# Half-row products of batches 2 to 7: stages A, D and C in one stretch each, with a value bank as the fourth place

## The chip, the cores and the metric

The program runs on one core of one Trainium2 chip. The metric is device time in microseconds, one execution at a time, as the median of the runs shown.

## The reference

```python
def _attn_ref(x):                       # x: 8 x 3072 x 256
    X = np.fft.fft(x, axis=1)
    X = np.fft.fft(X, axis=2)
    return X.real.astype(np.float32)

def _moe_ref(x, mu_k, mu_r, w_k, w_v, w_r):
    x_prev = np.concatenate([np.zeros((B, 1, D)), x[:, :-1, :]], axis=1)
    xk = mu_k * x + (1.0 - mu_k) * x_prev
    xr = mu_r * x + (1.0 - mu_r) * x_prev
    k = np.maximum(xk @ w_k, 0.0)
    v = k * k @ w_v
    return (1.0 / (1.0 + np.exp(-(xr @ w_r)))) * v
```

The output of the first function is the x of the second: a two-dimensional Fourier transform of each batch, of which the real part is kept, and then a channel mix with a squared ReLU (width 1024) and a sigmoid gate.

## The kernel before

**The main loop.** The channel mix of all eight batches is cut into 48 chunks of 512 positions, six to a batch, and each chunk into four steps, so that a batch has 24 steps. A step holds `k_piece` (four products of 512 columns with `wk`, line 825, then a ReLU by ACT, line 835), one `v_tile` (eight products of 256 columns with `wv`, line 866) and, every fourth step, `r_item` (eight products with `wr`, line 852, then a sigmoid by ACT). DVE squares the ReLU's result at every second step (line 845) and multiplies a finished value tile by the gate (`v_out`, line 888), which goes out by DMA.

**The transform of the next batch** is woven into these steps, in three stages. Stage A multiplies the folded input by a table `w_h` and makes `a`. Stage D multiplies `a` by `w_d` and makes `g_all`. Stage C multiplies `g_all` by `m_cs` and makes `pq`; DVE adds and subtracts its halves (`halves`). From batch 2 on (stage D: from batch 3 on) the products of these stages take only half of TensorE's rows: 48 or 64 of 128 rows, the lower half (`lo64`) or the upper one (`hi64`). They are issued alternately, lower and upper, and write different banks of one tile.

**PSUM.** Three tiles of two banks each (`psW0` to `psW2`, handed out in turn by `ps_w`) serve `k_piece`, `r_item` and all three stages; two tiles of one bank each (`psV0`, `psV1`, `ps_v`) serve the value tiles. A value bank takes two value tiles, `tb` 0 and 1 or `tb` 2 and 3, and is free when `v_out` has read it. A `psW` tile is free when ACT has copied it out (`evac`, line 574).

**The order** is written out by hand. `at(step, f, ...)` puts work at a step; `event(step, ...)` puts half-row products behind that step's `v_tile`; `v_behind(steps)` moves the `v_tile` of these steps up, ahead of their own `k_piece`. A step runs thus: `k_piece`, the small stage work, `v_tile`, the event, a `v_tile` that was moved up, DVE's `v_out` if the step stands in `OUT_FIRST`, the DVE work, `v_out` otherwise, the square. Every engine runs its instructions in exactly this order. For batch t of 3 to 7, with s = 24t - 48, the half-row products stand in four **stretches**, each between two stretches of ordinary 128-row products:

- s+29: the 2 leading products of stage A (line 603, all rows) and 46 half-row products (line 617), in three `psW` tiles
- s+33: 48 half-row products of stage D (line 679), three tiles
- s+37: the last 4 of stage D and 32 of stage C (line 746), three tiles
- s+41: 24 of stage C, and the first 16 of stage A of batch t+1, two tiles

Batch 2 has its own steps: 16 products of its stage A stand in a stretch at step 20 that stays for batch 1's stage C; then come stretches at 31 (A), 39 (C) and 41 (C, and batch 3's first 16 of A). Its stage D uses all rows.

Of the kernel before, what the change touches and what calls it, by code (L numbers as in the profile page):

```python
# [9 lines left out]
FP32 = mybir.dt.float32  # L10
FP16 = mybir.dt.float16
# [28 lines left out]
def kernel(  # L40
# [23 lines left out]
    y_pool = ctx.enter_context(tc.tile_pool(name="y_sb", bufs=1))  # L64
# [15 lines left out]

    def ps_v():
        return ps_slot("V", 2, 512)
# [22 lines left out]
    xp_t, xm_t, p_t, eo_t = {}, {}, {}, {}  # L105
    V = nc.vector
# [175 lines left out]
    lo64, hi64 = slice(0, 64), slice(64, 128)  # L282
# [15 lines left out]
    g_all = const.tile([P, NU // 2, 256], FP16)  # L298
# [4 lines left out]
    m_cs = const.tile([P, 3, NJ, 64], FP16)  # L303
# [81 lines left out]
    WA, WB = 4 * NU, 2 * NU  # L385
# [3 lines left out]
    w_h, w_h0 = w_hh[:, 0:WB], w_hh[:, WB:2 * WB]  # L389
# [150 lines left out]
    w_d = const.tile([P, 2, 64], FP16)  # L540
# [25 lines left out]
    a_t = {}  # L566
    y_t = {}
    x_t = {}

    def evac(out_ap, in_ap, eng):  # L570
        if eng == "V":
            V.tensor_copy(out=out_ap, in_=in_ap)
        else:
            nc.scalar.activation(out=out_ap, in_=in_ap, func=AF.Copy)  # L574

    def a_tile(b):
        a_t[b] = y_pool.tile([P, 2, NU, 64], FP16, name="a")
# [20 lines left out]

    def a_slot_0(b, e):
        a_ps[b, 1, e] = ps_w()
        nc.tensor.matmul(out=a_ps[b, 1, e][:, 2 * NU * 7:2 * NU * 8], lhsT=eo_t[b, 0][0:112, 0, e, :],
                         rhs=w_h0, start=True, stop=True)

    def a_slots_0(b):
        for e in range(2):
            a_slot_0(b, e)

    def a_half(b, h, e, eng="A"):  # L610
        if (h, e) == (0, 0):
            a_tile(b)
        ps = a_ps[b, h, e] if h else ps_w()
        for i in range(8):
            for g in range(h and i == 7, 2):
                rows = slice(64 * g, 64 * g + N1)
                nc.tensor.matmul(out=_v(ps, 512 * g + 2 * NU * i, [(1, 2 * NU)]),  # L617
                                 lhsT=eo_t[b, h][rows, i + 1 - h, e, :], rhs=w_h[rows],
                                 start=True, stop=True)
        evac(_v(a_t[b], 64 * NU * e + 8 * h, [(16, 2), (32, 2 * NU), (1, 8)]),  # L620
             _v(ps, 0, [(512, 2), (1, 2 * NU), (2 * NU, 8)]), eng)

    def a_sum(b, h, i0, eng="A", m=4):

# [19 lines left out]
    a_ps = {}  # L644
# [24 lines left out]
        d_units(b, ps, 4 * n, k, 512)  # L669
        d_evac(ps, 4 * n, k, 512, eng)  # L670

    def d_half(b, n, eng="A"):
        u0, k = 4 * n, min(4, NU // 2 - 4 * n)
        ps = ps_w()
        for i in range(k):
            for e in range(2):
                for g, rows in enumerate((lo64, hi64)):
                    o = 512 * g + 256 * e + 64 * i
                    nc.tensor.matmul(out=ps[:, o:o + 64],  # L679
                                     lhsT=a_t[b][rows, e, 2 * (u0 + i):2 * (u0 + i) + 2, :],  # L680
                                     rhs=w_d[rows, e], start=True, stop=True)
        evac(_v(g_all, 256 * u0, [(1, 2), (128, 2 * k), (2, 32)]),
             _v(ps, 0, [(512, 2), (32, 2 * k), (1, 32)]), eng)
        evac(_v(g_all, 256 * u0 + 64, [(128, 2), (256, k), (1, 64)]),
             _v(ps, 256, [(512, 2), (64, k), (1, 64)]), eng)

    def d_small(b, u, n, eng="A"):
        ps = ps_v()
# [34 lines left out]
    def c_tiles(b):  # L723
        y_t[b] = y_pool.tile([P, NSL + 1, 2, 64], FP16, name="y")
# [13 lines left out]
    def c_pairs(b, s0, n, eng="A"):  # L738
        if s0 == 0:
            c_tiles(b)  # L740
            y_t[b, "pq"] = y_pool.tile([P, 2 * NJ, 2, 64], FP16, name="pq")
        ps = ps_w()
        for f in range(2):
            for sl, i, rows, u in c_slots(s0, n):
                o = 512 * (sl % 2) + 128 * i + 64 * f
                nc.tensor.matmul(out=ps[:, o:o + 64], lhsT=g_all[rows, u, 128 * f:128 * f + 128],  # L746
                                 rhs=m_cs[rows, f, sl // 2], start=True, stop=True)
        evac(_v(y_t[b, "pq"], 128 * s0, [(256, n // 2), (128, 2), (1, 128)]),
             _v(ps, 0, [(128, n // 2), (512, 2), (1, 128)]), eng)

    def halves(b, lo, hi, hs=(0, 1)):
# [189 lines left out]
    w, first = ps_w(), ps_w()  # L941
# [15 lines left out]
    for a in range(2):  # L957
        t = x_t["t", a] = mix_pool.tile([P, 24, 64], FP16, name=f"t{a}")
# [8 lines left out]
    odd = ps_v()  # L967
# [14 lines left out]
    work = {}  # L982

    def at(step, f, *args):
        work.setdefault((step, "x" if f in (a_item, a_sum, d_item, d_small, c_item, c_tiles, turned, minus_0, r_item, quarter_tables) else "w"),
                        []).append((f, args))


# [76 lines left out]
    at(16, fold, 2, 0)  # L1065
    at(17, butterfly, 2, 0)
    event(18, (c_pairs, 1, 0, 8, "V"), (c_pairs, 1, 8, 8))
    event(20, (c_pairs, 1, 16, 8), (c_pairs, 1, 24, 4), (a_half, 2, 0, 0))
    v_behind(21)
    at(19, halves, 1, 0, 13)  # L1070
    at(20, diff, 1, 0, 12)
# [48 lines left out]
    for t in range(3, B):  # L1120
        s = 24 * t - 48

        def every(step, f, *args):
            at(s + step, f, t, *args)

        every(9, fold, 0)
        every(12, quarters_1, 0)
        every(13, quarters_2, 0)
        every(15, fold, 1)
        every(26, quarters_1, 1)  # L1130
        every(27, quarters_2, 1)
# [29 lines left out]
    for step in range(nk + LAG):  # L1161
# [3 lines left out]
        v = v_steps.get(step)  # L1165
# [52 lines left out]
```

## Time and profile before

| | |
|---|---|
| time, median of 3 runs | 427.71 us (427.27 to 428.07) |
| span of the profiled execution | 425.4 us |
| TensorE busy | 419.5 us (99%), granted clock 0.999 |
| DVE busy | 371.4 us (87%) |
| ACT busy | 327.2 us (77%) |

The profile is of one execution. Its span runs from the first to the last instruction; the measured time holds some 2.3 us more, which lie outside the span. In the views, a line such as L679 is a line of the kernel, `out<-in` names tiles, xN counts instructions, and "DVE" or "ACT" behind an arrow is the engine that ended a wait. A row of the chain of waits gives a start, a length and the instructions that held the end of the program during it.

### The profile page before, as it was taken

What the parts mean: (1) busy time and instruction counts of PE and PEld (TensorE: products, weight loads), DVE (VectorE), ACT (ScalarE), POOL (GpSimd) and SP (SyncE); (2) the same over time, 40 slices, a digit from 0 to 9 for tenths busy, and PEclk for the clock granted to TensorE, in tenths of its full rate; (3) what the DMA queues carried; (4) which work ended last, traced back from release to release, by engine and by line L of the source; (5) the groups of instructions that cost most, each with busy time, mean ns of one, the idle gap of its engine ahead of it and who ended that gap; (6) DMA issues with size and microseconds to landing.
All of it is one profiled execution on the core that took longest, in us unless ns stands there. A gap on an engine that the chain in (4) does not pass through costs nothing.

```text
span 425.4 us, 9649 instructions
## 1 busy us (share of the span) xinstructions
PE 419.5 (99%) x3991; PEld 294.6 (69%) x3991; DVE 371.4 (87%) x593; ACT 327.2 (77%) x407; POOL 64.3 (15%) x99
## 2 busy tenths in 40 slices
PE   8999999999999999999999999999999999999996
PEld 3767766776677767776767676777767776776765
DVE  8999999999998989989899898988899776977553
ACT  7889886797867986689767887678876798666661
POOL 7478500200060001400041000500000000000000
PEclk9999999999999999999999999999999999999999
DMA  8779972632385233932349232772223232332334
GB/s 173 109 118 185 228 158 57 117 87 55 73 161 137 52 76 57 217 97 51 75 79 216 55 73 55 140 169 57 68 59 74 54 74 52 74 70 55 76 74 101
DMA packets 35104, 42.08 MB, mean 99 GB/s; under 512 B 4114, under 2 KB 31092, under 8 KB 35060
## 3 DMA queue, kind: packets, MB, share of 16 engines
q1 hardware_dynamic: 27488, 25.41, 24.6%
q0 software_dynamic: 7264, 15.80, 21.5%
q8 instruction: 31, 0.51, 0.5%
q10 hardware_dynamic: 308, 0.26, 0.2%
q14 instruction: 13, 0.11, 0.1%
HBM read 32.08 MB, written 25.17 MB: 135 GB/s over the span
## 4 chain that ended last, share of the span: by engine, by line
PE 98%; DVE 1%; issue 0%; POOL 0%; ACT 0%; POOLq 0%
PE psW L825 39%; PE psV L866 37%; PE psW L852 10%; PE psV L878 3%; PE psW L746 2%; PE psW L617 1%; PE psW L679 1%; PE psW L235 1%; PE psW L635 1%; PE psW L657 1%; PE psV L378 1%; PE psW L714 0%; DVE rw L308 0%; PE psV L657 0%; PE psV L635 0%
## 5 line engine op out<-in xcount | busy, mean ns | idle before, releaser
L835 ACT ACTIVATE rl<-psW 128x1024 f16<-128x1024 f32 x192 | 193.7, 1032 | 82.3 <-PE psW L825 81.2
L825 PE MATMUL psW<-x,wk 128*128 128x512 f16 (+1 forms) x776 | 193.4, 377 | 0.3 <-DVE x L962 0.3
L866 PE MATMUL psV<-wv_sb,k 128*128 128x256 f16 x1424 | 184.3, 273 | 0.0
L866 PEld LDWEIGHTS <-k 128*128 128x128 f16 x1424 | 136.4, 98 | 38.3
L845 DVE TENSOR_TENSOR k<-rl 128x2048 f16<-128x2048 f16 (+1 forms) x100 | 115.6, 1157 | 26.3 <-ACT rl L835 26.0
L825 PEld LDWEIGHTS <-wk 128*128 128x128 f16 x776 | 75.6, 98 | 54.9 <-issue 0.4
L888 DVE SCALAR_TENSOR_TENSOR o<-psV,r 128x512 f32<-128x512 f32 (+1 forms) x97 | 65.7, 680 | 15.0 <-PE psV L866 14.1
L790 DVE TENSOR_TENSOR x<-y,t 128x1536 f16<-128x1536 f16 (+3 forms) x76 | 62.4, 827 | 2.2
L857 ACT ACTIVATE r<-psW 128x1024 f16<-128x1024 f32 x48 | 49.5, 1032 | 0.8 <-PE psW L852 0.8
L852 PE MATMUL psW<-wr,x 128*128 128x256 f16 x384 | 49.8, 273 | 0.0
L852 PEld LDWEIGHTS <-x 128*128 128x128 f16 x384 | 37.5, 98 | 14.2 <-issue 0.2
L574 ACT ACTIVATE g_all<-psW 128x512 f16<-128x512 f32 (+8 forms) x62 | 29.0, 542 | 1.3 <-PE psW L679 1.0
L574 ACT ACTIVATE a<-psW 128x832 f16<-128x832 f32 x31 | 25.4, 865 | 1.2 <-PE psW L617 1.2
L494 POOL IOTA gate<- 1x1 int32 x7 | 0.8, 121 | 163.8 <-DVE gate L493 163.8
L574 ACT ACTIVATE pq<-psW 128x1024 f16<-128x1024 f32 (+1 forms) x27 | 23.3, 917 | 1.5 <-PE psW L746 1.4
L141 POOL DMA_INDIRECT xm<-in_x_dram,idx_g x18 | 23.5, 1304 | 5.5 <-issue 5.5
L779 DVE TENSOR_SCALAR t<-d,muf_t 128x1536 f16<-128x1536 f16 (+3 forms) x44 | 21.8, 508 | 0.1
L172 DVE TENSOR_TENSOR p<-xp,xm 112x2304 f16<-112x2304 f16 (+6 forms) x19 | 21.7, 1141 | 0.1
L779 DVE TENSOR_SCALAR t<-d,mu_m 128x1536 f16<-128x1536 f16 x32 | 19.6, 612 | 0.0
L759 DVE TENSOR_TENSOR y<-pq 128x960 f16<-128x960 f16 (+3 forms) x28 | 15.8, 604 | 3.2 <-ACT pq L574 2.8
L767 DVE TENSOR_TENSOR d<-y 128x1664 f16<-128x1664 f16 (+5 forms) x19 | 16.7, 879 | 0.3 <-ACT y L574 0.2
L878 PE MATMUL psV<-wv_sb,k 128*128 128x256 f16 x112 | 14.7, 273 | 0.0
(148 smaller groups left out, 221.1 us busy)
## 6 DMA issues: line engine op xcount, KB each, us to landing
out_dram<-o SPq DMA_DIRECT2D x189, 128.0 KB, 2.4
xp<-in_x_dram POOLq DMA_DIRECT2D x12, 216.0 KB, 4.4
xp<-in_x_dram POOLq DMA_DIRECT2D x13, 192.0 KB, 6.9
xp<-in_x_dram POOLq DMA_DIRECT2D x2, 384.0 KB, 8.0
wv_sb<-in_moe_w_v_dram POOLq DMA_DIRECT2D x1, 512.0 KB, 8.3
xp<-in_x_dram SPq DMA_DIRECT2D x1, 480.0 KB, 4.2
xp<-in_x_dram POOLq DMA_DIRECT2D x1, 432.0 KB
xm<-in_x_dram,idx_g POOLq DMA_INDIRECT x18, 9.2
```

The lines of the kernel that those rows point to most:

```text
L141: nc.gpsimd.indirect_dma_start(dst, None, src, bass.IndirectOffsetOnAxis(ap=idx, axis=0))
L574: nc.scalar.activation(out=out_ap, in_=in_ap, func=AF.Copy)
L779: V.tensor_scalar(out=dst, in0=src, scalar1=mu, scalar2=None, op0=ALU.mult)
L790: V.tensor_tensor(out=_v(x_t[b, j, m], o, [(64 * step, hi - lo), (step, 64)]), in0=y_t[b][:, lo + 3 * m:hi + 3 * m, a], in1=x_t["t", a][:, ...
L825: nc.tensor.matmul(out=st["k", ds][:, 512 * hs + lo:512 * hs + hi], lhsT=wk_sb[m][a][:, 128 * fc:128 * fc + 128], rhs=xk[:, a, 512 * i + l ...
L835: nc.scalar.activation(out=st["rl"][:, 2 * ds:2 * ds + 2], in_=st["k", ds].rearrange("p (f t) -> p f t", f=2), func=AF.Relu, bias=0.0, sca ...
L845: V.tensor_tensor(out=k2_t[c][:, lo:hi], in0=r, in1=r, op=ALU.mult)
L852: nc.tensor.matmul(out=ps[:, 256 * tb:256 * tb + 256], lhsT=x_t[b, 1, m][:, a, 512 * i + 128 * tb: 512 * i + 128 * tb + 128], rhs=wr_sb[m] ...
L857: nc.scalar.activation(out=st["r", c], in_=ps, func=AF.Sigmoid)
L866: nc.tensor.matmul(out=st["v", tb - h][:, 256 * h:256 * h + 256], lhsT=k2_t[c][:, fc, 128 * tb:128 * tb + 128], rhs=wv_sb[:, fc], start=(f ...
L878: nc.tensor.matmul(out=st["v", tb - h][:, 256 * h:256 * h + 256], lhsT=k2_t[c][:, fc, 128 * tb:128 * tb + 128], rhs=wv_sb[:, fc], start=fc ...
L888: V.scalar_tensor_tensor(out=o.rearrange("p a b -> p (a b)")[:, 0:256 * n], in0=st["v", t0][:, 0:256 * n], scalar=16.0, in1=st["r", c][:, ...
```

## The change

Each of the stages A, D and C of a batch gets one stretch: A (62 products) at s+29, D (52) at s+33, C (54) at s+37; the stretch at s+41 goes, and so does batch 2's at 41. One stage needs more than three `psW` tiles hold, so the rest of its products goes to a fourth place, the value bank that is not being filled at that time (`v_bank`). That bank is taken without moving the count that hands out value banks, so the next pair of value tiles gets the same bank. The products that write its lower-half part stand first in the stretch, and are copied out during it; those of its upper-half part stand last, and are copied out third, ahead of the last `psW` tile. All these copies are ACT's. The two leading products of stage A (`a_slot_0`) move to an earlier step, in a tile of their own with an evacuation of their own. The two products for a slot of stage C that is not used are left out, and `turned` runs once a batch and not in two parts. `v_out` moves ahead of the other DVE work at the steps s+28, s+32, s+36 and at step 30.

```diff
+    def v_bank():
+        k = ps_n["V"] % 2
+        return psum.tile([P, 512], FP32, name=f"psV{k}", tag=f"psV{k}", bufs=1)
+
+    def side_by_side(lo, hi, n, f):
+        for k in range(max(len(lo), len(hi))):
+            if k == n:
+                f()
+            for items in (lo, hi):
+                for out, w, r in items[k:k + 1]:
+                    nc.tensor.matmul(out=out, lhsT=w, rhs=r, start=True, stop=True)
...
+        lo, hi = both(0), both(1)
+        side_by_side(run(v, 0, 0, 1, 12, 15) + lo,
+                     hi + run(v, 3 * WB, 1, 1, 12, 16) + run(v, 7 * WB, 1, 0, 15, 16),
+                     3, lambda: out(v, 0, 1, 12, 3, (0,)))
+        out(ws[0], 0, 0, 0, 9)
+        out(ws[1], 0, 1, 0, 9)
+        out(v, 3 * WB, 1, 12, 4, (1,))
+        out(v, 7 * WB, 0, 15, 1, (1,))
+        out(ws[2], 0, 0, 9, 6)
+        out(ws[2], 6 * WB, 1, 9, 3)
...
+    def d_all(b):
+        ws = [ps_w() for _ in range(3)]
+        v = v_bank()
...
+        def out(ps, n, k, gs=(0, 1), o=0, e=256):
+            g, m = gs[0], len(gs)
+            evac(_v(g_all, 1024 * n + g, [(1, m), (128, 2 * k), (2, 32)]),
+                 _v(ps, o, [(512, m), (32, 2 * k), (1, 32)]), "A")
+            evac(_v(g_all, 1024 * n + 64 + 128 * g, [(128, m), (256, k), (1, 64)]),
+                 _v(ps, o + e, [(512, m), (64, k), (1, 64)]), "A")
+
+        side_by_side(run(0, 3) + run(0, 0) + run(0, 1) + run(0, 2),
+                     run(1, 0) + run(1, 1) + run(1, 2) + run(1, 3),
+                     2, lambda: out(v, 3, 1, (0,), 0, 64))
+        out(ws[0], 0, 4)
+        out(ws[1], 1, 4)
+        out(v, 3, 1, (1,), 128, 64)
+        out(ws[2], 2, 4)
...
+        side_by_side(run(1, 3) + run(1, 0) + run(1, 1) + run(1, 2),
+                     run(0, 0) + run(0, 1) + run(0, 2) + run(0, 3), 2,
+                     lambda: evac(_v(pq, 128 * 25, [(1, 128)]), _v(v, 128, [(1, 128)]), "A"))
+        out(0)
+        out(1)
+        evac(_v(pq, 128 * 24, [(256, 2), (1, 128)]), _v(v, 0, [(256, 2), (1, 128)]), "A")
+        out(2)
...
-    OUT_FIRST = (12, 20, 28, 36, 38, 40)
+    OUT_FIRST = (12, 20, 28, 30, 36, 38, 40, *(24 * t - 48 + k for t in range(3, B) for k in (28, 32, 36)))
...
-    event(31, (a_slots_0, 2), (a_half, 2, 1, 0), (a_half, 2, 1, 1), (a_half, 2, 0, 1))
+    at(22, a_slot_0, 2)
+    event(31, (a_all, 2))
...
-    event(39, (c_pairs, 2, 0, 8), (c_pairs, 2, 8, 8))
-    event(41, (c_pairs, 2, 16, 8), (c_pairs, 2, 24, 4), (a_half, 3, 0, 0))
-    v_behind(42)
+    event(39, (c_all, 2))
+    v_behind(40)
...
-        event(s + 29, (a_slots_0, t), (a_half, t, 1, 0), (a_half, t, 1, 1), (a_half, t, 0, 1))
-        event(s + 33, (d_half, t, 0), (d_half, t, 1), (d_half, t, 2))
-        at(s + 36, turned, 0, 12)
-        event(s + 37, (d_half, t, 3), (c_pairs, t, 0, 8), (c_pairs, t, 8, 8))
-        at(s + 39, turned, 12, 13)
-        event(s + 41, (c_pairs, t, 16, 8), (c_pairs, t, 24, 4),
-              *([(a_half, t + 1, 0, 0)] if t + 1 < B else ()))
-        v_behind(s + 30, s + 34, s + 35, s + 38, s + 42)
+        at(s + 18, a_slot_0, t)
+        event(s + 29, (a_all, t))
+        event(s + 33, (d_all, t))
+        at(s + 36, turned, 0, 13)
+        event(s + 37, (c_all, t))
+        v_behind(s + 30, s + 34, s + 35, s + 38)
```

**ACT, stage D of batch 5.** Before, between the ReLU of step s+33 and that of s+34 (numbers are buffers):

```order
L835 ACTIVATE rl_3710<-psW0_3740 128x1024
L574 ACTIVATE g_all_148<-psW1_3755 128x2x8x32
L574 ACTIVATE g_all_148<-psW1_3755 128x2x4x64
L574 ACTIVATE g_all_148<-psW2_3774 128x2x8x32
L574 ACTIVATE g_all_148<-psW2_3774 128x2x4x64
L574 ACTIVATE g_all_148<-psW0_3793 128x2x8x32
L574 ACTIVATE g_all_148<-psW0_3793 128x2x4x64
L835 ACTIVATE rl_3710<-psW1_3823 128x1024
```

The same place in the changed kernel:

```order
L903 ACTIVATE rl_3725<-psW2_3755 128x1024
L574 ACTIVATE g_all_148<-psV1_3773 128x2x32
L574 ACTIVATE g_all_148<-psV1_3773 128x64
L574 ACTIVATE g_all_148<-psW0_3770 128x2x8x32
L574 ACTIVATE g_all_148<-psW0_3770 128x2x4x64
L574 ACTIVATE g_all_148<-psW1_3771 128x2x8x32
L574 ACTIVATE g_all_148<-psW1_3771 128x2x4x64
L574 ACTIVATE g_all_148<-psV1_3773 128x2x32
L574 ACTIVATE g_all_148<-psV1_3773 128x64
L574 ACTIVATE g_all_148<-psW2_3772 128x2x8x32
L574 ACTIVATE g_all_148<-psW2_3772 128x2x4x64
L903 ACTIVATE rl_3725<-psW0_3847 128x1024
```

Two pairs of 64-column evacuations of the value bank have come in, one ahead of the first `psW` tile and one behind the second.

**PE, stage D of batch 5.** The `k_piece` of step s+34 ends and the value tile of step s+35 begins, in the changed kernel:

```order
L893 MATMUL psW0_3847<-x00_3418,wk00_95 128x512
L893 LDWEIGHTS wk01_96
L893 MATMUL psW0_3847<-x00_3418,wk01_96 128x512
L934 LDWEIGHTS k2_3563
L934 MATMUL psV1_3853<-wv_sb_103,k2_3563 128x256
```

This value tile takes the bank `psV1` that the stretch used (`psV1_3773` above). Between the stretch and it stand the value tile of step s+34, which goes on in the other bank, and the `k_piece` of s+34. Behind the stretches of A and C, and behind those of batch 2, at least two `k_piece`s stand there beside the value tile.

**DVE, batch 2, step 30.** Before:

```order
L845 TENSOR_TENSOR k_1299<-rl 128x2048
L779 TENSOR_SCALAR t_1370<-d,muf_t 128x768
L790 TENSOR_TENSOR x_1256<-y,t_1370 128x768
L888 SCALAR_TENSOR_TENSOR o<-psV_1343,r 128x512
L779 TENSOR_SCALAR t_1454<-d,mu_m 128x1536
```

In the changed kernel:

```order
L913 TENSOR_TENSOR k_1285<-rl 128x2048
L956 SCALAR_TENSOR_TENSOR o<-psV_1329,r 128x512
L847 TENSOR_SCALAR t_1360<-d,muf_t 128x768
L858 TENSOR_TENSOR x_1242<-y,t_1360 128x768
L847 TENSOR_SCALAR t_1459<-d,mu_m 128x1536
```

`v_out` (line 888, now 956) has moved ahead of the step's scaling and mixing. At step 38, ahead of stage C of batch 2, DVE's order is as it was.

More of the change, by code (lines that the diff above doesn't have):

```diff
@@ L597, in a_item @@
              _v(ps, 0, [(1, WA), (128, 8)]), eng)
[L601 to L606, printed above, removed]
-        for e in range(2):
[L608 to L621, printed above, removed]
+    def v_bank():
+        k = ps_n["V"] % 2
+        return psum.tile([P, 512], FP32, name=f"psV{k}", tag=f"psV{k}", bufs=1)
@@ new lines, in side_by_side, with a_slot_0 @@
+    def side_by_side(lo, hi, n, f):
[5 more added lines that the diff above has]
+                    nc.tensor.matmul(out=out, lhsT=w, rhs=r, start=True, stop=True)
+    def a_slot_0(b):
+        a_tile(b)
+        ps = ps_w()
+        for e in range(2):
+            nc.tensor.matmul(out=ps[:, WB * e:WB * e + WB], lhsT=eo_t[b, 0][0:112, 0, e, :],
+                             rhs=w_h0, start=True, stop=True)
+        evac(_v(a_t[b], 15, [(64 * NU, 2), (32, WB)]), _v(ps, 0, [(WB, 2), (1, WB)]), "A")
@@ new lines, in a_all, with run, both, out @@
+    def a_all(b):
+        ws = [ps_w() for _ in range(3)]
+        v = v_bank()
+        def run(bank, o, g, e, lo, hi):
+            rows = slice(64 * g, 64 * g + N1)
+            return [(_v(bank, o + WB * k, [(1, WB)]),
+                     eo_t[b, q // 8][rows, q % 8 + 1 - q // 8, e, :], w_h[rows])
+                    for k, q in enumerate(range(lo, hi))]
+        def both(g):
+            return (run(ws[0], 512 * g, g, 0, 0, 9) + run(ws[1], 512 * g, g, 1, 0, 9)
+                    + run(ws[2], 512 * g, g, 0, 9, 15) + run(ws[2], 512 * g + 6 * WB, g, 1, 9, 12))
+        def out(ps, o, e, q, n, gs=(0, 1), step=512):
+            evac(_v(a_t[b], 64 * NU * e + 16 * gs[0] + q, [(16, len(gs)), (32, WB), (1, n)]),
+                 _v(ps, o, [(step, len(gs)), (1, WB), (WB, n)]), "A")
+        lo, hi = both(0), both(1)
[8 more added lines that the diff above has]
+        out(ws[2], 6 * WB, 1, 9, 3)
@@ L670, in d_item, with run @@
         d_evac(ps, 4 * n, k, 512, eng)
[L672 to L685, printed above, removed]
+    def d_all(b):
+        ws = [ps_w() for _ in range(3)]
+        v = v_bank()
+        def run(g, n):
+            rows = (lo64, hi64)[g]
+            ps, o, step = (ws[n], 512 * g, 256) if n < 3 else (v, 128 * g, 64)
+            return [(ps[:, o + step * e + 64 * i:o + step * e + 64 * i + 64],
+                     a_t[b][rows, e, 2 * u:2 * u + 2, :], w_d[rows, e])
+                    for i, u in enumerate(range(4 * n, min(4 * n + 4, NU // 2))) for e in range(2)]
+        def out(ps, n, k, gs=(0, 1), o=0, e=256):
[11 more added lines that the diff above has]
+        out(ws[2], 2, 4)
     def d_small(b, u, n, eng="A"):
@@ L749, in c_pairs, with c_all, run, out @@
              _v(ps, 0, [(128, n // 2), (512, 2), (1, 128)]), eng)
+    def c_all(b):
+        c_tiles(b)
+        y_t[b, "pq"] = y_pool.tile([P, 2 * NJ, 2, 64], FP16, name="pq")
+        ws = [ps_w() for _ in range(3)]
+        v = v_bank()
+        def run(odd, n):
+            got = []
+            for sl, i, rows, u in c_slots(8 * n, 8 if n < 3 else NSL - 24):
+                if sl % 2 == odd:
+                    ps, o = (ws[n], 512 * odd + 128 * i) if n < 3 else (v, 128 * (sl - 24))
+                    got += [(ps[:, o + 64 * f:o + 64 * f + 64],
+                             g_all[rows, u, 128 * f:128 * f + 128], m_cs[rows, f, sl // 2])
+                            for f in range(2)]
+            return got
+        pq = y_t[b, "pq"]
+        def out(n):
+            evac(_v(pq, 1024 * n, [(256, 4), (128, 2), (1, 128)]),
+                 _v(ws[n], 0, [(128, 4), (512, 2), (1, 128)]), "A")
+        side_by_side(run(1, 3) + run(1, 0) + run(1, 1) + run(1, 2),
[5 more added lines that the diff above has]
+        out(2)
     def halves(b, lo, hi, hs=(0, 1)):
@@ L984, in at @@
     def at(step, f, *args):
-        work.setdefault((step, "x" if f in (a_item, a_sum, d_item, d_small, c_item, c_tiles, turned, minus_0, r_item, quarter_tables) else "w"),
+        work.setdefault((step, "x" if f in (a_item, a_sum, d_item, d_small, c_item, c_tiles, turned, minus_0, r_item, quarter_tables, a_slot_0) else "w"),
                         []).append((f, args))
@@ L1067 @@
     event(18, (c_pairs, 1, 0, 8, "V"), (c_pairs, 1, 8, 8))
-    event(20, (c_pairs, 1, 16, 8), (c_pairs, 1, 24, 4), (a_half, 2, 0, 0))
+    event(20, (c_pairs, 1, 16, 8), (c_pairs, 1, 24, 4))
     v_behind(21)
```

## The prediction

> **What bounds the kernel now.** First the page: busy times, and the engines' shares of the chain that ended last.
>
> ```profile
> span 425.4 us, 9649 instructions
> PE 419.5 (99%) x3991; PEld 294.6 (69%) x3991; DVE 371.4 (87%) x593; ACT 327.2 (77%) x407; POOL 64.3 (15%) x99
> PE 98%; DVE 1%; issue 0%; POOL 0%; ACT 0%; POOLq 0%
> ```
>
> TensorE works without a break, and the chain is TensorE's own queue. So a piece of its work removed is time won, and a wait put into its queue is time lost, at full price: no idle time absorbs either. Then the chain of waits over batch 5's transform, for the price of a stretch (start, length, what).
>
> ```profile
> 229.96 0.77 PE psV L866 x7
> 230.72 0.05 PE psW L603 x2
> 230.77 0.71 PE psW L617 x46
> 231.48 0.98 PE psV L866 x8
> ...
> 238.53 0.87 PE psV L866 x8
> 239.41 0.81 PE psW L679 x48
> 240.21 0.98 PE psV L866 x8
> ...
> 245.53 0.02 PE psW L695
> ...
> 248.17 0.16 PE psW L679 x4
> 248.33 0.48 PE psW L746 x32
> 248.81 0.98 PE psV L866 x8
> ...
> 256.76 0.46 PE psW L746 x24
> 257.22 0.20 PE psW L617 x16
> 257.42 0.98 PE psV L866 x8
> ```
>
> Eight value products take 0.87, but 0.98 right behind each stretch: leaving one costs 0.11. Inside, 16 products of A in the middle of a run take 0.20, that is 0.025 for a lower and an upper one together; 32 of C take 0.48, 0.029 to 0.030 a pair. D's 24 pairs at 0.029 are 0.70 of 0.81 + 0.11 = 0.92, so entering and leaving cost 0.22. The other three give the same: 0.16 + 0.48 + 0.11 less 18 pairs, 0.23; 0.46 + 0.20 + 0.11 less 12 x 0.029 and 8 x 0.025, 0.22; A's 0.71 + 0.11 less 24 x 0.025 (its last two run alone), 0.22.
>
> **The change: what TensorE saves.** Six stretches go, one in each of batches 2 to 7: 6 x 0.22 = 1.32. One `turned` goes in five batches, 0.02 each by L695: 0.10. The two products of C fewer save nothing: before, C is 28 pairs; now 26 pairs and two upper products that run alone. D stays at 26 pairs, A at 32 such times, and the two leading products of A only move. **Sum: 1.42 us won**, or 0.24 a batch, if nothing waits.
>
> **Stage D, batches 3 to 7: what the value bank costs.** Timeline of TensorE and ACT at this place before (start, length).
>
> ```profile
> 239.34 0.87 PE L679 MATMUL psW<-w_d,a 64*128 64x64 f16 x48
> 240.14 1.05 PE L866 MATMUL psV<-wv_sb,k 128*128 128x256 f16 x8
> 241.03 1.03 PE L825 MATMUL psW<-x,wk 128*128 128x512 f16 x4
> 241.89 1.04 PE L866 MATMUL psV<-wv_sb,k 128*128 128x256 f16 x8
> 238.57 1.02 ACT L835 ACTIVATE rl<-psW 128x1024 f16<-128x1024 f32 x1 [0.67 <-PE psW L825]
> 239.79 3.36 ACT L574 ACTIVATE g_all<-psW 128x512 f16<-128x512 f32 x6 [0.20 <-PE psW L679]
> 242.96 2.93 ACT L835 ACTIVATE rl<-psW 128x1024 f16<-128x1024 f32 x3
> ```
>
> I count from the stretch's first product, S = 239.34. ACT starts its first copy at S + 0.45, when the first tile is full, and takes 242.96 - 239.79 = 3.17 for three tiles, 1.06 each. Small evacuations, start to start, stand in these rows.
>
> ```profile
> 231.12 2.38 ACT L574 ACTIVATE a<-psW 128x832 f16<-128x832 f32 x3 [0.21 <-PE psW L617]
> 233.36 1.96 ACT L835 ACTIVATE rl<-psW 128x1024 f16<-128x1024 f32 x2
> 248.37 0.45 ACT L574 ACTIVATE g_all<-psW 128x128 f16<-128x128 f32 x2
> 248.70 1.95 ACT L574 ACTIVATE pq<-psW 128x1024 f16<-128x1024 f32 x2
> L574 ACT ACTIVATE g_all<-psW 128x128 f16<-128x128 f32 x10 | 2.2, 293 | 0.1
> ```
>
> A pair of 128 columns takes 0.33; 832 columns take (233.36 - 231.12) / 3 = 0.75, so a column is some 0.83 ns and a pair of 64 columns 0.33 - 2 x 64 x 0.00083 = 0.22. The last of a pair ends 0.12 after ACT could start its next (0.293 long, 0.165 apart).
>
> Now the changed order. Two products for the value bank lead the lower half, so the first tile is full 2 x 0.029 later, S + 0.51; the bank's first pair is copied before that (ACT is free from 239.47, and two products are done at about S + 0.28), and costs nothing. ACT then copies two tiles until S + 0.51 + 2.12 = S + 2.63, then the bank's second pair: free at 2.63 + 0.22 + 0.12, about S + 2.97. TensorE: 26 pairs instead of 24, so the value tile of s+34 starts at S + 0.80 + 0.06 = 0.86, the `k_piece` at 0.86 + 0.89 = 1.75, the value tile of s+35, which needs that bank, at 1.75 + 0.86 = S + 2.61. **Wait: 0.36, with the hand-over some 0.39 us a batch.** Before, this value tile waited for `v_out` alone, long done. Queued behind it are the `k_piece`s of s+35 and s+36, hence ACT's ReLUs, and all of TensorE: full price, 5 x 0.39 = 1.95. The wait is a difference of a sum of ACT rows and a sum of TensorE rows; 0.10 either way covers both (0.28 to 0.50).
>
> The `k_piece` at 1.75 needs the first tile, copied by S + 0.51 + 1.06 + 0.12 = 1.69: just free.
>
> The Trainium skill ("TensorEngine Tiling (Array Packing)", PSUM Bottleneck) says that packing the array speeds TensorE up but not the copy out of PSUM, which may become the bottleneck. The rows agree in stage D, 3.17 of ACT for 0.81 of TensorE; if it held in all three stages, the third rival below would come.
>
> **Stages A and C: covered.** Two `k_piece`s stand there between, so the bank is wanted at S + 0.91 + 0.88 + 2 x 0.86 = S + 3.5. ACT in A: two tiles of 936 columns at 0.83 each from S + 0.53, then 208 and 52 columns, 0.22 + 0.09, free at 2.6. In C two of 0.90 from 0.51 and 256 columns, free at 2.7. The first tiles are wanted at 1.8 and free at 1.5. Tightest is the bank itself: its upper-half products come at S + 0.7 and wait for the copy of its lower-half part, done at 0.6 to 0.65. That margin, 0.05 to 0.1, is a thing to watch in all three stages.
>
> The bank's first product also waits for `v_out` on DVE. In batch 5's stage A (S about 230.65) DVE's square ends its turn at the start of the next row, 229.21; `v_out` is put there now, takes 0.68, and is done at 229.9. Covered by 0.7.
>
> ```profile
> 228.07 1.22 DVE L845 TENSOR_TENSOR k<-rl 128x2048 f16<-128x2048 f16 x1
> 229.21 0.61 DVE L779 TENSOR_SCALAR t<-d,mu_m 128x1536 f16<-128x1536 f16 x1
> ```
>
> **Batch 2: DVE is late.** The busy times of one window (length; PE, PEld, DVE, ACT), and the timeline at the start of its stages C and A.
>
> ```profile
> 77.66:101.30 23.64, 23.64 (x255) 17.07 (x253) 23.30 (x35) 18.68 (x23) 2.45 (x4) 1.00 0.46 96
> 100.64 0.68 DVE L888 SCALAR_TENSOR_TENSOR o<-psV,r 128x512 f32<-128x512 f32 x1
> 100.74 0.64 PE L746 MATMUL psW<-m_cs,g_all 64*128 64x64 f16 x32
> 82.10 0.41 DVE L779 TENSOR_SCALAR t<-d,muf_t 128x768 f16<-128x768 f16 x1
> 82.66 0.22 PE L603 MATMUL psW<-w_hh,eo 112*128 112x52 f16 x2
> ```
>
> DVE is busy for 23.30 of these 23.64 us, and `v_out` ahead of stage C runs from 100.64 to 101.32, where stage C starts at 100.74. Now C needs the bank that this `v_out` reads: its first product comes no earlier than 101.32, 0.58 late. Since DVE's queue has no slack, the end of this `v_out` is fixed, and the smaller wait at stage A (`v_out` from 82.10 to 82.78 against a first product at about 82.6) is not paid twice. DVE may run ahead by what TensorE saved at step 20 (16 products, 0.2): 0.38 to 0.58, I take 0.50. From there the stretch at 41 is saved (0.22), but here an `r_item` and not a `k_piece` comes second and the third tile is wanted at S + 3.5, free at 3.6: 0.09. **Batch 2: +0.50 + 0.09 - 0.22 = +0.37.**
>
> **Sum.** Batches 3 to 7: 5 x (0.39 - 0.24) = +0.75; batch 2 +0.37; together +1.1, with the tight margin of the bank's two halves not counted. Span 425.4 + 1.1 = 426.5; the median of the runs lies 2.3 above the span, so 428.8; I say **428.9**. With the bounds: 0.28 and 0.38 give +0.45, 0.50 and 0.58 give +1.75: 428.1 to 429.5.
>
> **The rivals.** (1) *The wait in D is mostly hidden*: ACT's small copies overlap more than two 128-column ones do, or begin sooner. With 0.2 a batch: 5 x (0.2 - 0.24) + 0.37 = +0.2, 427.9, no change. For it: ACT's rows spread by 0.03 a copy; against: 0.2 off needs a whole pair to cost nothing. 0.18. (2) *The saving comes through, faster*: neither D nor batch 2 waits, 427.71 - 1.42 = 426.3; with batch 2's wait alone, 426.9. It needs the bank free before the `k_piece` ends, against the order of the copies. 0.08. (3) *Copying out rules in A and C as well*: the copies of 52, 104 and 156 columns write scattered runs of one to three elements, and if a lower-half copy takes 0.1 longer, the upper-half products wait 0.1 in all 16 stretches: +1.6 more, 430.4. It decides from a copy 0.05 to 0.1 longer than the columns say. 0.12. That the stretches would be broken by other work is excluded by the order of the instructions.
>
> **How the numbers follow.** Forecast 0.62, of which 0.10 lies within 0.2% (0.86 us, about what a measurement of this kernel can tell from no change) and 0.52 above. Slower by over 0.2%: 0.52 + 0.12 = 0.64. Within: 0.10 + 0.18 = 0.28. Faster: 0.08. Range 427.6 to 430.2: the bounds above, with most of rival 1 below and half of rival 3 above.
>
> **What would show it.** In the changed profile: three stretches a batch, with 0.98 behind each; in stage D a wait of TensorE of some 0.4 at the value tile of s+35, ended by ACT's copy of `psV` into `g_all`; the same at no place of A and C; at batch 2 a wait of 0.4 to 0.6 for `v_out` ahead of stage C. TensorE's busy time should hardly rise, its idle time should, by about 2.5 in all. The forecast is wrong if the value tile of s+35 starts less than 2.7 after the stretch's first product, or if waits appear inside the stretches.

## The result, and the profile after

| | before | after |
|---|---|---|
| median of the runs compared | 427.71 us (5 runs) | 429.68 us (5 runs, 429.18 to 429.81) |
| ratio after / before | | 1.0046, 95% interval 1.0034 to 1.0058 |
| span of the profiled execution | 425.4 us | 428.0 us |

The change costs about 2.0 us, where 1.2 was forecast. (The span rose by 2.6. The time of an execution lies 1.8 above its own span in after, 429.81 against 428.0, and not 2.3; by that the execution profiled before took 425.4 + 1.8 = 427.2, less than the median.) Two lines of the page of after: busy times, and the engines' shares of the chain that ended last.

```profile
PE 420.0 (98%) x3974; PEld 294.0 (69%) x3974; DVE 371.3 (87%) x593; ACT 334.0 (78%) x442; POOL 63.5 (15%) x99
PE 79%; DVE 13%; ACT 5%; issue 2%; POOL 0%; DVEq 0%; POOLq 0%
```

Before, 98% of the chain was TensorE. Now DVE and ACT hold 18% of it: whenever TensorE waits, the chain goes over to the engine that it waits for and stays there until that engine itself waited for TensorE. TensorE's own busy time rose by 0.5 us, though 1.42 of its work was to go (part of a wait counts as busy here: below, 0.45 from start to start leaves 0.29 of idle time). Its idle time rose from 5.9 to 8.0, by 2.1 where 2.5 was forecast.

The chain of waits over batch 5's transform (start, length, what):

```profile
232.75 0.62 PE psW L611 x50
...
233.53 0.98 PE psV L934 x8
...
240.62 1.02 ACT rl L903
241.65 2.75 ACT g_all L574 x8
244.41 0.04 issue
244.45 1.03 PE psV L934 x8
...
250.88 0.67 PE psW L611 x46
...
251.64 0.98 PE psV L934 x8
```

Three stretches are left, with 0.98 behind A's and C's, as forecast (a chain row of a stretch names only part of its products; single rows between are left out). In stage D the chain runs through ACT: its eight copies into `g_all` end, and the value tile starts. The same place by time, TensorE first, then ACT (start, length; in brackets the idle time by the modelled end of the product before):

```profile
242.25 1.05 PE L934 MATMUL psV<-wv_sb,k 128*128 128x256 f16 x8
243.13 1.03 PE L893 MATMUL psW<-x,wk 128*128 128x512 f16 x4
244.45 1.03 PE L934 MATMUL psV<-wv_sb,k 128*128 128x256 f16 x8 [0.29 <-ACT g_all L574]
```

```profile
241.65 0.34 ACT L574 ACTIVATE g_all<-psV 128x64 f16<-128x64 f32 x2
241.88 2.28 ACT L574 ACTIVATE g_all<-psW 128x512 f16<-128x512 f32 x4
244.01 0.39 ACT L574 ACTIVATE g_all<-psV 128x64 f16<-128x64 f32 x2
244.22 1.26 ACT L574 ACTIVATE g_all<-psW 128x512 f16<-128x512 f32 x2
```

A `k_piece` followed at once takes 0.86, so the value tile could have started at 243.13 + 0.86 = 243.99. It starts at 244.45, 0.05 after the third row of ACT has ended (244.01 + 0.39): a wait of 0.45, in each of batches 3 to 7. (TensorE's waits below are counted in this way, from start to start; the brackets show less, since the ends are modelled.)

Batch 2 around stage A, TensorE, ACT and DVE:

```profile
82.17 1.04 PE L934 MATMUL psV<-wv_sb,k 128*128 128x256 f16 x8
83.31 0.18 PE L611 MATMUL psV<-w_hh,eo 48*128 48x52 f16 x1
...
85.13 1.03 PE L893 MATMUL psW<-x,wk 128*128 128x512 f16 x4
86.00 1.04 PE L920 MATMUL psW<-wr,x 128*128 128x256 f16 x8
87.36 1.02 PE L893 MATMUL psW<-x,wk 128*128 128x512 f16 x4 [0.33 <-ACT a L574]
```

```profile
83.81 1.97 ACT L574 ACTIVATE a<-psW 128x936 f16<-128x936 f32 x2
85.64 0.63 ACT L574 ACTIVATE a<-psV 128x208 f16<-128x208 f32 x2
85.95 1.36 ACT L574 ACTIVATE a<-psW 128x624 f16<-128x624 f32 x2
```

```profile
82.57 0.69 DVE L956 SCALAR_TENSOR_TENSOR o<-psV,r 128x512 f32<-128x512 f32 x1
```

Two waits stand here. In batch 5, where nothing waits, the first product of a stretch starts 0.97 after the value tile ahead of it. Here it takes 83.31 - 82.17 = 1.14: A's first product waits 0.17 for the `v_out` that ends at 82.57 + 0.69 = 83.26. (In the traces of e5 to e8 and e11 this wait is 0.08.) The third user of `psW` behind the stretch, the `k_piece` of step 33, could start at 86.00 + 0.87 and starts at 87.36: 0.49 late, because the third tile's two copies end at 87.31. The forecast gave the first no price and does not have the second. Ahead of stage C of batch 2, DVE and then TensorE:

```profile
96.83 0.69 DVE L956 SCALAR_TENSOR_TENSOR o<-psV,r 128x512 f32<-128x512 f32 x1 [0.47 <-PE psV L934]
...
101.67 0.68 DVE L956 SCALAR_TENSOR_TENSOR o<-psV,r 128x512 f32<-128x512 f32 x1
```

```profile
100.99 1.04 PE L934 MATMUL psV<-wv_sb,k 128*128 128x256 f16 x8
102.41 0.19 PE L611 MATMUL psV<-m_cs,g_all 64*128 64x64 f16 x1 [0.38 <-DVE o L956]
```

C's first product comes 102.41 - 100.99 = 1.42 after its value tile and not 0.97: 0.45 late, for the `v_out` at 101.67, as forecast. But the `v_out` before that one waited 0.47 itself, at 96.83, for a value tile: DVE, which was said to have no slack, stood still there.

**Where the time went, by steps.** The traces here reach the `k_piece` of step 31 up to 0.6 us apart. So I compare the starts of the same `k_piece`s in each trace: from step 31 to step 44 (stages A, D and C of batch 2) and from step 44 to step 164, divided by five (batches 3 to 7). The last column has the median and ratio of the runs. One run of e2, the profiled one, took 2474.82 us and one of e11 728.43; both are left out, and e2 has no step times for that reason.

| kernel | steps 31 to 44 | a batch of 3 to 7 | median, ratio to before |
|---|---|---|---|
| before | 29.06 | 50.238 | |
| after | 30.04 | 50.507 | 429.68, 1.0046 |
| e4_v_out_first_alone | 29.06 | 50.238 | 427.80, 1.0003 [0.9994, 1.0012] |
| e1_bank_second | 30.05 | 50.064 | 427.48, 0.9994 [0.9985, 1.0004] |
| e2_batch2_as_before | | | 428.87, 1.0026 [1.0017, 1.0035] |
| e3_both | 28.91 | 50.063 | 426.76, 0.9975 [0.9965, 0.9985] |
| e5_third_tile_early | 29.95 | 50.063 | 427.42, 0.9997 [0.9988, 1.0006] |
| e6_quarters_later | 29.52 | 50.061 | 426.72, 0.9987 [0.9978, 0.9996] |
| e7_both_in_batch_2 | 29.50 | 50.064 | 426.98, 0.9987 [0.9978, 0.9996] |
| e8_even_runs | 30.54 | 50.515 | 430.16, 1.0061 [1.0047, 1.0075] |
| e9_five_and_four | 31.00 | 50.894 | 432.51, 1.0127 [1.0111, 1.0142] |
| e11_no_wait_in_A | 29.46 | 50.062 | 426.71, 0.9985 [0.9976, 0.9994] |
| e10_no_wait_in_batch_2 | 29.19 | 50.060 | 426.33, 0.9977 [0.9968, 0.9986] |

Before itself had medians of 427.73 beside e1 to e4, 427.32 beside e5 to e8, 427.31 beside e9 to e11. Two shifts have to be taken out. Batch 2's 16 leading products of A moved from step 20 into the first column, net 0.15 (steps 20 to 24 take that much less in after); batch 3's moved from the first column into the second, net 0.15 too (16 x 0.0125 less 0.05 for its `a_slot_0` at step 42). So batch 2 costs 30.04 - 29.06 - 0.15 + 0.15 = 0.98 more, and batches 3 to 7 together 5 x 0.269 - 0.15 = 1.20, or 0.24 each. The sum is 2.2 us. The first column is good to about 0.1, by one pair: the trace of e12, which is e10's kernel up to its last product, gives 29.10 for e10's 29.19.

### The profile page after: what moved, and what is told of

It reads as the page before. It is cut to its first block, busy times and chain, and to the rows that moved or that the text cites. A ratio compares the mean times of both kernels' runs of the same rounds, so it can differ in the third digit from the quotient of the medians.

```text
span 428.0 us, 9650 instructions
## 1 busy us (share of the span) xinstructions
PE 420.0 (98%) x3974; PEld 294.0 (69%) x3974; DVE 371.3 (87%) x593; ACT 334.0 (78%) x442; POOL 63.5 (15%) x99
## 4 chain that ended last, share of the span: by engine, by line
PE 79%; DVE 13%; ACT 5%; issue 2%; POOL 0%; DVEq 0%; POOLq 0%
PE psW L893 32%; PE psV L934 31%; PE psW L920 8%; ACT g_all L574 3%; DVE k L913 3%; DVE o L956 2%; PE psW L611 2%; DVE x L858 2%; DVE t L847 2%; ACT rl L903 1%; DVE p L172 1%; PE psW L235 1%; DVE eo L211 1%; PE psV L946 1%; PE psV L611 1%
## 5 line engine op out<-in xcount | busy, mean ns | idle before, releaser
L574 ACT ACTIVATE a<-psW 128x936 f16<-128x936 f32 (+4 forms) x37 | 29.8, 851 | 0.4 <-PE psW L662 0.4
L574 ACT ACTIVATE g_all<-psW 128x512 f16<-128x512 f32 (+5 forms) x47 | 26.3, 635 | 0.3 <-PE psW L684 0.2
L574 ACT ACTIVATE pq<-psW 128x1024 f16<-128x1024 f32 (+1 forms) x21 | 20.4, 1007 | 0.1
```

## The experiments

**e1: the value bank copied out second.** In stage D alone, of after:

```diff
         out(ws[0], 0, 4)
-        out(ws[1], 1, 4)
         out(v, 3, 1, (1,), 128, 64)
+        out(ws[1], 1, 4)
         out(ws[2], 2, 4)
```

> The changed kernel, with one thing altered: in stage D of batches 3 to 7 the bank's upper-half part is copied out second, ahead of the second psW tile, and not third. Theory (TensorE waits 0.45 us a batch at the value tile of s+35 for that copy alone): the copy ends about 1.06 us sooner, before the value tile comes, so the five waits go and no other takes their place: 429.7 - 5 x 0.45 = 427.4 us, and no wait over 0.1 in stage D. Rival (ACT has more copies than stage D can hide, whatever their order): the wait moves to the k_piece of s+35, behind the second tile: 429.2 to 429.7 us.

Measured: 427.48. The same place in batch 5, TensorE and ACT:

```profile
242.16 1.03 PE L893 MATMUL psW<-x,wk 128*128 128x512 f16 x4
243.03 1.04 PE L934 MATMUL psV<-wv_sb,k 128*128 128x256 f16 x8
```

```profile
240.91 1.19 ACT L574 ACTIVATE g_all<-psW 128x512 f16<-128x512 f32 x2
241.99 0.35 ACT L574 ACTIVATE g_all<-psV 128x64 f16<-128x64 f32 x2
242.20 2.30 ACT L574 ACTIVATE g_all<-psW 128x512 f16<-128x512 f32 x4
```

The value tile follows its `k_piece` after 0.87. A batch takes 0.443 less than in after: the whole wait, and no other has come. Moving two copies of 64 columns ahead of two of 512 wins the 2.2 us back.

**e2 and e3: batch 2 in the four stretches of before**, e2 on after and e3 on e1. The old functions stand beside the new ones.

```diff
-    OUT_FIRST = (12, 20, 28, 30, 36, 38, 40, *(24 * t - 48 + k for t in range(3, B) for k in (28, 32, 36)))
+    OUT_FIRST = (12, 20, 28, 36, 38, 40, *(24 * t - 48 + k for t in range(3, B) for k in (28, 32, 36)))
...
-    event(20, (c_pairs, 1, 16, 8), (c_pairs, 1, 24, 4))
+    event(20, (c_pairs, 1, 16, 8), (c_pairs, 1, 24, 4), (a_half, 2, 0, 0))
...
-    at(22, a_slot_0, 2)
-    event(31, (a_all, 2))
+    event(31, (a_slots_0, 2), (a_half, 2, 1, 0), (a_half, 2, 1, 1), (a_half, 2, 0, 1))
...
-    event(39, (c_all, 2))
-    v_behind(40)
+    event(39, (c_pairs, 2, 0, 8), (c_pairs, 2, 8, 8))
+    event(41, (c_pairs, 2, 16, 8), (c_pairs, 2, 24, 4))
+    v_behind(42)
```

> The changed kernel for batches 3 to 7; batch 2 in its stretches of before (20, 31, 39, 41, three psW tiles, no value bank, v_out of step 30 not moved), but without batch 3's products at 41. Theory (batch 2's waits of 0.17, 0.49, 0.45 and 0.12 us come from its value bank and its bigger copies): those 1.2 us go, one stretch of 0.22 comes back: 429.7 - 1.0 = 428.7 us. Rival (DVE and ACT are late at batch 2 anyway and the wait only moves to a later place of the batch): 429.5 us or more.

> Both alterations together: batch 2 as before and the bank's upper-half part copied out second in stage D. Theory: what is left is the saving of a stretch and one turned in five batches, 5 x 0.24 = 1.2 us, against waits of 0.02 in stage A: 427.7 - 1.1 = 426.6 us, faster than before. Rival (a longer stretch costs TensorE as much as the one saved): 427.7 us.

Measured 428.87 and 426.76: by the medians batch 2's part of the change costs 0.7 to 0.8 (0.98 by the steps), about twice the +0.37 of the forecast or more. e3 is faster than both kernels (0.25% below before).

**e4: `v_out` moved ahead, and nothing else**, in before.

```diff
-    OUT_FIRST = (12, 20, 28, 36, 38, 40)
+    OUT_FIRST = (12, 20, 28, 30, 36, 38, 40, *(24 * t - 48 + k for t in range(3, B) for k in (28, 32, 36)))
```

> The kernel before, with only the list of steps at which v_out goes ahead of DVE's other work as in the change. Theory (DVE's order costs nothing by itself): 427.7 us. Rival (the scaling and mixing that now come 0.7 us later make TensorE wait at a k_piece or r_item): 428.5 us or more.

Measured 427.80; both step times are those of before to 0.01. The moved `v_out`s cost nothing.

**e5: the third tile of stage A earlier**, e1 with this in batch 2 alone:

```diff
-        out(v, 3 * WB, 1, 12, 4, (1,))
-        out(v, 7 * WB, 0, 15, 1, (1,))
         out(ws[2], 0, 0, 9, 6)
         out(ws[2], 6 * WB, 1, 9, 3)
+        out(v, 3 * WB, 1, 12, 4, (1,))
+        out(v, 7 * WB, 0, 15, 1, (1,))
```

> e1_bank_second with, in batch 2 alone, the third psW tile of stage A copied out ahead of the value bank's upper pieces. The copy of the third tile then ends 0.31 us earlier (the two pieces took 0.216 and 0.093), so the 0.49 wait at the k_piece of step 33 should fall to 0.18. Theory (the v_out that stage C of batch 2 waits for is late because its value tile was late, so the wait in A is paid again in C): v_out moves with TensorE, C's wait stays at 0.45, and the whole 0.31 is won: 427.2 us, against 427.5 for e1_bank_second. Rival (the prediction's: the end of that v_out is fixed by DVE's own queue): C's wait grows to 0.76 and nothing is won, 427.5.

The time, 427.42, is the rival's, but neither mechanism came. TensorE (line numbers are 4 higher from here on in this kernel):

```profile
86.86 1.02 PE L897 MATMUL psW<-x,wk 128*128 128x512 f16 x4
88.17 0.61 PE L688 MATMUL psW<-w_eo,a 128*128 128x128 f16 x8 [0.29 <-ACT rl L907]
```

The `k_piece` is 0.04 late, and the next user of `psW`, the `d_item`, waits 0.45 for ACT's ReLU, which stands behind A's copies. ACT owes more copies here than TensorE gives it time for; their order only chooses who waits. C's wait stayed at 0.45. So this run doesn't tell the two theories of C's wait apart.

**e6: work moved out of DVE's way**, e1 with batch 3's `quarters_2` of the first half one step later, behind the `v_out`; **e7** has e5's edit as well.

```diff
-        every(13, quarters_2, 0)
+        every(14 if t == 3 else 13, quarters_2, 0)
```

> e1_bank_second with, for batch 3's first half alone, quarters_2 (three DVE instructions, 1.75 us) two steps... issued at step 38 behind that step's v_out in place of step 37 ahead of it. Theory: DVE's work ahead of the v_out of step 38 is what makes stage C of batch 2 wait; the v_out ends 1.8 us earlier, the 0.45 wait ahead of C is gone and A's 0.49 stays: 427.0 us. Rival: DVE has no slack anywhere, so a later value tile or k piece waits for DVE in C's place, 427.3 to 427.5.

> e5_third_tile_early and e6_quarters_later together. Theory: the two are apart and add, 0.31 + 0.45 off e1_bank_second's 427.5: 426.7 us, with 0.18 left in A and none ahead of C; as fast as e3_both, which has batch 2 in the four stretches of before. Rival: one of the two covers for the other, 427.0.

In e6 the wait ahead of C is gone and A's stays at 0.50; steps 31 to 44 take 0.53 less (0.45, and 0.09 less ahead of A's first product), and no other wait came. e7 is no better than e6, for e5's reason: its `d_item` waits 0.44.

**e8 and e9: the price of stage A's copies.** Each copy of nine slots in two, in e8 eight and one, in e9 five and four; both on e1.

```diff
-        out(ws[0], 0, 0, 0, 9)
-        out(ws[1], 0, 1, 0, 9)
+        for e in range(2):
+            out(ws[e], 0, e, 0, 8)
+            out(ws[e], 8 * WB, e, 8, 1)
```

> e1_bank_second with each of stage A's two copies of nine slots (936 columns, runs of nine) split into one of eight slots (832 columns) and one of one slot (104 columns). If an odd run costs as much as the next even one: 0.745 + about 0.13 = 0.87 for the pair, less than the 0.90 to 0.93 of the one copy, although there is one instruction more, and the third tile's wait in batch 2 falls by about 0.1: 427.4 us. If a copy costs by its columns: 0.80 + 0.13 = 0.93 or more, and the wait grows: 427.6 us.

> e1_bank_second with each of stage A's copies of nine slots split into one of five and one of four, where e8 split them into eight and one. Theory (a copy into stage A's tile costs at least about 4.2 ns for each of its 104 runs, and about 0.90 ns a column where a run is longer than that; from 104 runs of 3 in 0.434 us, 52 runs of 4 in 0.216, 104 runs of 6 in 0.563, of 8 in 0.76): five and four cost 0.47 + 0.44 = 0.91 us, no more than the one copy of nine (0.905 and 0.934), so the time stays at e1_bank_second's 427.5, and the third tile's wait at 0.5. Rival (each instruction more costs 0.13 to 0.3, which would also explain e8's 2.7): 0.2 to 0.3 more for each pair, waits of 0.1 and 0.35 in stage A of every batch as in e8, about 430.0.

ACT in batch 3's stage A, e8 and then e9 (a row takes instructions on one tile together, whatever their widths):

```profile
132.51 2.60 ACT L574 ACTIVATE a<-psW 128x832 f16<-128x832 f32 x4
134.60 0.97 ACT L574 ACTIVATE a<-psV 128x208 f16<-128x208 f32 x2
```

```profile
132.59 2.96 ACT L574 ACTIVATE a<-psW 128x520 f16<-128x520 f32 x4
135.28 0.73 ACT L574 ACTIVATE a<-psV 128x208 f16<-128x208 f32 x2
```

In after the two copies of nine took 85.64 - 83.81 = 1.83. The same columns take 2.09 in e8, with 0.3 more passed on to the copy behind, and 2.69 in e9, where 0.91 a pair had been expected. Behind stage A of every batch TensorE then waits 0.12 + 0.34 (e8) and about 0.31 + 0.53 (e9). Both theories of e8 fell, the floor for each run in e9 as well: five and four, with fewer columns in each, are dearer than eight and one.

**e12: the copies by themselves.** Behind e10's work, four more products fill one `psW` tile, and ACT then repeats one copy of it six times for each of 24 forms. In the code, `q` is the first slot, `n` the number of slots, and `dst` and `src` are the patterns that the expectation names.

```diff
+    for q, n, kind in ((0, 9, ""), (0, 8, ""), (0, 5, ""), (5, 4, ""), ...
...
+        for k in range(6):
+            evac(_v(a_t[B], q, dst), _v(ps, 0, src), "A")
```

> e10_no_wait_in_batch_2 with extra work behind its last product, so its time is longer by some 60 to 90 us and says nothing: ScalarE copies one psW tile into an unused tile of stage A's form, six times each in 24 forms (first slot and number of slots a run; 104 runs of f16, 64 bytes from row to row; source strided as in stage A, and some with the source or the destination contiguous). Read is the steady time from start to start. Known from the kernels: nine slots from slot 0 0.905 to 0.934 us, eight from 0 0.76, six from 9 0.56, three from 9 0.43, five from 0 0.52 to 0.59, four from slot 5 0.79 (e9). Theory 1 (a run that crosses 16 bytes costs an access more): four from 5 and four from 6 0.79, four from 4, from 0, from 1 and from 12 about 0.44, nine from 0 0.9, eight from 1 about 1.1. Theory 2 (a run that begins at an odd slot costs as if filled to whole pairs, or more): four from 5 and four from 1 0.79, four from 6 0.44. Theory 3 (no form is dear by itself; e9's 0.79 is the cost of writing next to what the copy before it just wrote): four slots cost about 0.44 from every slot. In all of them the destination sets it: with a contiguous destination four slots cost about 0.40 and nine about 0.85, and with a contiguous source what they cost with the strided one.

The one run took 530.62 us, some 103 more than before. Each repetition waits for the one before, so a row gives whole durations, and not the times from start to start of the expectation. The stretches of four repetitions each (length, ACT busy; then TensorE's granted clock, the DMA share and GB/s, which say nothing here): nine slots from slot 0 and eight from 0; then four from 5, six from 9, four from 4, three from 9, four from 6 and one from 0; then eight from 1 and four from 1; then two from 0 and three from 0; then four from 5 with a contiguous source; last four and nine with a contiguous destination.

```profile
422.65:426.94 4.29, 4.17 (x4) 0.58 0.01 4
428.92:432.49 3.57, 3.46 (x4) 0.50 0.00 0
...
438.25:442.53 4.28, 4.16 (x4) 0.50 0.00 0
444.12:447.02 2.90, 2.77 (x4) 0.50 0.00 0
448.16:450.34 2.18, 2.07 (x4) 0.50 0.00 0
451.42:454.02 2.60, 2.49 (x4) 0.50 0.00 0
455.23:457.43 2.20, 2.08 (x4) 0.50 0.00 0
458.50:461.10 2.60, 2.49 (x4) 0.50 0.00 0
...
477.36:482.56 5.20, 5.08 (x4) 0.50 0.00 0
484.53:487.14 2.61, 2.50 (x4) 0.50 0.00 0
...
493.06:494.55 1.49, 1.38 (x4) 0.50 0.00 0
495.59:498.20 2.61, 2.49 (x4) 0.50 0.00 0
...
503.65:507.92 4.27, 4.16 (x4) 0.50 0.00 0
...
515.99:518.18 2.19, 2.07 (x4) 0.50 0.00 0
519.72:523.64 3.92, 3.81 (x4) 0.50 0.00 0
```

A quarter of the busy time is one copy. With a contiguous destination four slots (416 columns) take 0.52 and nine (936) 0.95: 0.17 + 0.00083 a column. Eight from 0 (0.865), six from 9 (0.69), four from 4 and from 6 (0.52) and two from 0 (0.345) cost just that. One slot (0.62), three from 0 or from 9 (0.62) and four from 1 (0.625) all cost more than their columns, 0.26, 0.43 and 0.52. Four from 5 cost 1.04, twice the contiguous copy, and with a contiguous source as well: the destination sets it. Theory 3 falls; of theories 1 and 2 each holds in part. A reading that fits 23 of the 24: where a run holds half of a 4-byte word, every piece of 16 bytes (eight slots, from slot 0 or 8) that it touches costs at least 4.2 to 4.3 ns ((0.62 - 0.17) / 104), and runs of whole words go by columns. Nine from 0 touch two such pieces, 2 x 4.2 x 104 + 170 = 1.04, as measured. Eight from 1 (1.27) cost more than that and stay open, and so does why.

The Trainium skill ("SBUF — State Buffer", Specifications) says that accesses go by 16-byte lines, that a line needs two hits for full bandwidth, and that each crossing pays a penalty. The runs agree that one slot in a line is dear (0.62) and, for runs with half a word, that 16 bytes are a border (four from 1 against four from 5, 0.625 and 1.04). They differ elsewhere: three slots from 0 pay (0.62) where two do not (0.345), though they hit their line more often, and four from 6 cross to a new line and pay nothing (0.52). So here the half word decides.

**e11 and e10: batch 2 without the wait in A.** e1 with a value tile ahead of the third user of `psW`; e10 has e6's edit as well.

```diff
-    at(33, d_item, 2, 0)
-    at(34, d_item, 2, 1)
+    at(34, d_item, 2, 0)
+    at(35, d_item, 2, 1)
...
-    at(35, d_item, 2, 2)
+    at(36, d_item, 2, 2)
...
-    at(32, r_item, (1, 0, 1))
-    at(36, d_item, 2, 3)
-    at(37, turned, 0, 13)
+    at(34, r_item, (1, 0, 1))
+    at(37, d_item, 2, 3)
+    at(38, turned, 0, 13)
```

> e1_bank_second with batch 2's r_item of step 32 issued at step 34, its four d_items one step later each (34 to 37) and its turned at step 38 in place of 37, so that a value tile stands ahead of the third user of psW behind stage A and ahead of the first reader of all of A's copies. The 0.49 wait in A should be gone and none take its place. Theory (A's wait is paid a second time in C): the wait of stage C for v_out stays between 0.45 and 0.55, and 0.4 to 0.5 is won: 427.0 us. Rival (the prediction's: that v_out's end is fixed by DVE's queue): C's wait grows to 0.9, nothing is won, 427.5.

> e11_no_wait_in_A with quarters_2 of batch 3's first half at step 38 as in e6. Theory: all of batch 2's waits over 0.2 are gone, 0.45 of A and 0.45 of C off e1_bank_second: 426.5 us, below e3_both's 426.8, in which batch 2 has its four stretches of before. Rival: DVE, 0.45 less late and with no slack, makes a later product wait: 427.0.

e11 ahead of stage C, DVE and then TensorE:

```profile
95.69 0.69 DVE L956 SCALAR_TENSOR_TENSOR o<-psV,r 128x512 f32<-128x512 f32 x1
...
100.54 0.68 DVE L956 SCALAR_TENSOR_TENSOR o<-psV,r 128x512 f32<-128x512 f32 x1
```

```profile
99.96 1.04 PE L934 MATMUL psV<-wv_sb,k 128*128 128x256 f16 x8
101.27 0.19 PE L611 MATMUL psV<-m_cs,g_all 64*128 64x64 f16 x1 [0.27 <-DVE o L956]
```

A's wait of 0.49 is gone; one of 0.10 came at the moved `r_item`, where none was expected. If the end of `v_out` were fixed, C's wait would have grown to 0.9; it shrank to 0.34 (101.27 - 99.96 - 0.97), below the 0.45 to 0.55 of the theory, the `v_out` at 95.69 no longer waits for its value tile, and steps 31 to 44 take 0.59 less. A's wait had been paid a second time in C. The 0.34 that is left is DVE's own work: e10, with e6's edit, has no wait there, and takes 29.19. By its ratio to before it is as fast as e3 (0.9977 and 0.9975, on different chips; by the steps it is some 0.1 slower), so what three stretches save in batch 2 is about paid by what remains of its waits (0.16 at the most at one place).

## Why the prediction was right, and where it was off

The forecast was 428.9 in a range of 427.6 to 430.2; 429.68 came, slower for the reason given: the value tile of s+35 starts 244.45 - 241.38 = 3.07 behind the stretch's first product, well over the 2.7 named as the sign. But the cost was 2.0 (2.2 by the steps) for 1.2, and 429.68 lies above the 429.5 that the sum's own bounds allow. It is inside the range only by the half of the third rival's price that was added on top, and that rival cost 0.1 of its 1.6; that the range held is in part luck. Point by point:

- **The stretches.** Right: A's and C's have 0.98 behind them (D's is not on the chain). So, nearly, is the saving of 0.24 a batch: e1, in which nothing but 0.02 in A waits, takes 50.238 - 50.064 = 0.174 less a batch, 0.03 more by the shift named above and 0.02 more without that wait, 0.22 (0.24 forecast; five times 0.02 is 0.1 of the error).
- **Stage D.** The mechanism and the place were right; e1 takes away the named order, and the wait goes with it. The size was 0.45 for 0.39: ACT's second bank pair ended 3.02 behind the stretch's start, not 2.97, and the hand-over took 0.05, not 0.03. Five times 0.06 is 0.3 of the error.
- **Stages A and C, batches 3 to 7.** Covered, as said. The tight margin of the bank's two halves is just used up in A (0.02 a batch). The third rival had this mechanism right, in A alone and at a fifth of its price.
- **Batch 2, stage A: the step that failed.** The forecast counted a wait for the third tile in C (0.09; 0.12 came) and called A covered for all batches. But in batch 2 an `r_item` stands second behind A's stretch too, so the third tile is wanted at S + 3.56 (86.00 + 0.87, with S = 83.31). At the prediction's prices (0.53, two copies of 0.83, 0.22 and 0.09, then 624 and 312 columns, about 0.58 + 0.32 + 0.12) it would have been free at about S + 3.5, just in time; the copies took until S + 4.00 (87.31 - 83.31), 0.49 behind with the hand-over. The mis-sized terms are the two copies of nine slots (0.94 and 0.90 from start to start) and the last two copies (1.36 to their end, for 1.02). e12 shows why for nine slots and for three from slot 9, which cost more than their columns. Six from 9 cost no more by themselves; in after they take 0.70 from start to start behind the one-slot copy, and 0.56 in e5, where a copy of nine stands ahead. No run has A's copies at whole words in these four places, so that the wait would be gone with them is not shown.
- **Batch 2, stage C.** The wait for `v_out` was 0.45 for 0.50. The step "the end of this `v_out` is fixed", so that nothing "is paid twice", was wrong: DVE's queue is full only as long as its inputs come, and a value tile that came late behind A made DVE late by at least as much. e11 shows it; e6 shows that DVE's work ahead of this `v_out` is the other half of the cause.

The sum: +0.75 forecast for batches 3 to 7 and 1.20 measured (D 0.3, A 0.1 and the smaller saving 0.1 more, to the rounding); +0.37 for batch 2 and 0.98 measured (A's wait 0.49, and 0.17 that A's first product waits for its `v_out`, which the forecast left out as not paid twice; 0.05 less ahead of C). The first rival needed a wait of 0.2 in D, the second none; neither came.

## What to carry to other kernels

When a buffer becomes the scratch place of another stage, list who takes it next and at what time, and copy it out in that order, not in the order in which it fills: here the place of two small copies was worth 2.2 us. A queue that is 99% busy is not thereby fixed in time: a wait upstream moves it, so a late buffer can be paid for at every meeting of the two engines. Try to split a stage over buffers along whole words and 16-byte borders of the destination: copies of nine slots cost 1.04 here where their columns make 0.95, and of eight just their columns. No run here tried such a split, and cutting the nine into eight and one (e8) lost 2.7 us.

## What was not expected of the hardware

A ScalarE copy that writes 104 runs of f16 cost 0.52 us for four slots from slot 0, 4, 6 or 12, 0.625 from slot 1 and 1.04 from slot 5; a single slot cost 0.62, as much as five from slot 0. In a chain of copies part of this shows only in the next one's start: in e8 the copies behind a one-slot copy took about 0.3 us more from start to start than the same copies elsewhere.
